# Second score pass of each head on half of the array's rows, one query block per half

## The chip, the core and the metric

The kernel runs on one core of a Trainium2 chip. The metric is the device time of one execution in microseconds (us); runs of the same kernel are summarised by their median. One profiled execution of the kernel gives the trace from which all rows come. TensorE is shown as two lines there: PE for the matmuls and PEld for the loads of the stationary operand ahead of each matmul. DVE is VectorE, ACT is ScalarE, POOL is GpSimd, SP is the queue that issues most DMAs.

## The reference: windowed attention, then a dense pair of layers

```
scores = (q @ k.T) / 8                       # batch 4, 8 heads, 768 positions, head size 64
keep   = (key < n_sink) | (0 <= query - key < window)    # 4 sinks, window 128
a      = softmax(where(keep, scores, -1e9))
x      = (a @ v) laid out as [3072 tokens, 512]
h      = x @ w_in                            # 512 -> 2048
out    = (max(h, 0) + log1p(exp(-|h|))) @ w_out   # 2048 -> 512
```

All inputs and outputs are float32.

## The kernel before

**Tiling.** The 3072 tokens are cut into 12 chunks of 256 (three per batch), each of two query blocks of 128 (`CH = 2`, index j). A chunk goes through eight heads of attention and then through eight slices of the dense layers. The attention of a chunk and the dense slices of the chunk before it are interleaved, so that each step holds one head and one slice.

**Precision.** Matmuls run on float32r, a rounded form of float32. To keep the accuracy, an operand is split into a high part (the rounded value) and a low part (what rounding left), and the products high·high, low·high and high·low are added up. The dense layers do this with three matmuls per tile (lines 495 and 546 to 548).

**The scores.** The head size is 64, and the array contracts over 128 rows, so the first two chunks (`EXACT = 2`) take plain float32 in another layout (line 257), while from the third chunk on a head's keys and queries are loaded twice, into rows 0 to 63 and into rows 64 to 127 of one tile of 656 columns (`load`, line 200): 400 columns of keys (previous block, sinks, own block, sinks, next block) and 256 columns of queries. `split` (line 204) then makes three things. ACT rounds the whole tile into `qkh` (line 210). DVE replaces the queries in the lower 64 rows of `qkh` by their low part (line 211, one subtraction of 64x256), so that a query column holds the high part over the low part. DVE writes the low part of the keys into `kl` on all 128 rows (line 213, 128x400). All these subtractions carry line 56, that of the helper `_sub`.

`scores` (line 246) then takes two passes for each query block j into the block's own PSUM tile `s`:

```
nc.tensor.matmul(s[:, :w], hi[:, st], hi[:, mv], start=True, stop=False)   # line 260
nc.tensor.matmul(s[:, :w], hi[:, st], kl[:, mv], start=False, stop=True)   # line 261
```

Line 260 gives (high + low query) times high key, line 261 gives (high + low query) times low key. Each is one weight load of 128 columns and one matmul that streams 264 columns, or 136 where j is the first block of a sequence (24 of 160 blocks). The order on PE is j=0 first and second pass, then j=1 first and second pass. With 10 chunks of 8 heads there are 80 heads, 160 matmuls of each line.

**What sets the order.** All engines issue in the order in which the program is emitted. The first two chunks and the preparation of the dense weights follow a list written out by hand (`START`). Then each step runs a fixed string of letters (`STEADY`): `k` sink weights, `W` the transposes of the softmax weights (line 329), `R`, `q`, `p` the `split` of the next head, `U` the 24 up-projection matmuls (line 495), `K` the sink transposes (line 313, every fourth step), `F`, `S` the scores, `T` the softmax, `D` six down-projection matmuls (lines 546 to 548), `P`, `N`, `V` the values (lines 362 and 369), `O`, `E` six more down-projection matmuls. So the scores stand between the up projection and the first half of the down projection, and the `split` of a head is emitted one step ahead of its scores.

**The softmax** (line 264) starts on DVE with a predicated copy that folds the window's two key blocks of `s` (line 275), then adds mask and scale (line 281). The PSUM pool of `s` has two tiles, one per block, so a head's scores wait for the softmax of the head before, a step earlier.

**A matmul of another shape.** In the constants, ahead of the first scores, line 113 spreads the two sizes over all partitions with a matmul whose stationary operand has one row. Around it stand the warm-up matmuls of line 660 (128 rows, on a tile of zeros) and the first scores of line 257 (128 rows).

Of the kernel before, what the change touches and what calls it, by code (L numbers as in the profile page):

```python
# [20 lines left out]
B, H, S, D = 4, 8, 768, 64  # L21
DM, DFF = 512, 2048
P = 128
# [3 lines left out]
CH = 2  # L27
CT = CH * P
KC = CH * KW + P
# [16 lines left out]
def _copy(nc, eng, out, in_):  # L46
    if eng == "A":
        nc.scalar.copy(out, in_)  # L48
    elif eng == "V":
        nc.vector.tensor_copy(out, in_)  # L50
    else:
        nc.gpsimd.tensor_scalar(out, in_, 1.0, 0.0, ALU.mult, ALU.add)


def _sub(nc, eng, out, a, b):
    (nc.vector if eng == "V" else nc.gpsimd).tensor_tensor(out, a, b, ALU.subtract)  # L56


def _zero(nc, out, finite):
    nc.gpsimd.tensor_scalar(out, finite, 0.0, 0.0, ALU.mult, ALU.add)  # L60
# [67 lines left out]
class _Attention:  # L128
# [75 lines left out]
    def split(self, h):  # L204
        if self.exact:
            return
        c, nc, chunk = self.c, self.c.nc, self.chunk
        r = self.heads[h]
        hi = c.lp.tile([P, QK], F32R, tag="qkh", name=f"qkh{chunk}_{h}")
        _copy(nc, c.E["qkh"], hi[:], r[:])  # L210
        _sub(nc, c.E["ql"], hi[D:, KC:], r[D:, KC:], hi[D:, KC:])
        kl = c.lp.tile([P, KC], F32R, tag="kl", name=f"kl{chunk}_{h}")
        _sub(nc, c.E["kl"], kl[:], r[:, :KC], hi[:, :KC])
        self.heads[h] = (hi, kl)
# [27 lines left out]
    def lone(self, j):  # L242

        return self.first and j == 0

    def scores(self, h):
        c, nc = self.c, self.c.nc
        ops = self.heads.pop(h)
        for j in range(CH):
            pool, tag = (c.ps_h, "h") if self.chunk == 0 and h % 2 else (c.ps_s, "s")  # L250
            s = pool.tile([P, 2 * P + NS], F32, tag=tag, name=f"s{self.chunk}_{h}_{j}")
            w = KW if self.lone(j) else 2 * P + NS
            mv = slice(j * KW, j * KW + w)
            st = slice(KC + j * P, KC + j * P + P)
            if self.exact:
                q, k = ops
                nc.tensor.matmul(s[:, :w], q[:, j * P : j * P + P], k[:, mv], start=True, stop=True)  # L257
            else:
                hi, kl = ops
                nc.tensor.matmul(s[:, :w], hi[:, st], hi[:, mv], start=True, stop=False)  # L260
                nc.tensor.matmul(s[:, :w], hi[:, st], kl[:, mv], start=False, stop=True)  # L261
            self.s[h, j] = s

    def softmax(self, h):
        c, nc, chunk = self.c, self.c.nc, self.chunk
        g, hh = h // G, h % G
        if hh == 0:
            self.a[g] = c.ap.tile([P, G, CH, KW], F32, tag="a", name=f"a{chunk}_{g}")
            self.rc[g] = c.sp.tile([P, CH, G], F32, tag="rc", name=f"rc{chunk}_{g}")
        sm = c.sp.tile([P, CH], F32, tag="sm", name=f"sm{chunk}_{h}")  # L270
        self.sm[h] = sm
        for j in range(CH):
            if self.lone(j):
                continue
            nc.vector.copy_predicated(self.s[h, j][:, :P], c.diag[:], self.s[h, j][:, KW:])
        for j in range(CH):
            a = self.a[g][:, hh, j]
            k = (chunk * H + h) * CH + j
            nm = c.stats[:, k : k + 1]
            m = c.masks[min(self.i0 + j, 2)]  # L280
            nc.vector.tensor_tensor_reduce(a, self.s.pop((h, j))[:, :KW], m[:], -SCALE, BIG, ALU.add, ALU.min, nm)  # L281
            nc.scalar.activation(a, a, AF.Exp, bias=nm, scale=-1.0, accum_out=sm[:, j : j + 1])  # L282
# [558 lines left out]
def _general(c):  # L841

    tc, nc = c.tc, c.nc
    with ExitStack() as st:
        pool = lambda n, bufs: st.enter_context(tc.tile_pool(name=n, bufs=bufs))
        psum = lambda n, bufs: st.enter_context(tc.tile_pool(name=n, bufs=bufs, space=bass.MemoryType.PSUM))
        c.stg, c.gp, c.xp, c.mp = pool("gstg", 2), pool("gp", 1), pool("gxp", 1), pool("gmp", 1)
        c.ps_acc, c.ps_h, c.gs, c.gt, c.gx = psum("gacc", 1), psum("gh", 1), psum("gs", 1), psum("gt", 1), psum("gx", 1)
        _general_weights(c)
        keep = _general_masks(c)  # L850
        with tc.For_i(0, B, 1) as b:
            for n in range(NCH):
                xh, xl = c.x[n] = [c.xp.tile([P, 4, CT], F32R, tag=f"x{e}", name=f"gx{e}{n}") for e in "hl"]
                for h in range(H):
                    if h % 2 == 0:
                        xt = c.gx.tile([P, CT], F32, name=f"g_x{n}_{h}", tag="g_x")
                    _general_head(c, b, n, h, keep, xt)
                    if h % 2 == 1:
                        _copy(nc, "A", xh[:, h // 2], xt[:])
                        _sub(nc, "V", xl[:, h // 2], xt[:], xh[:, h // 2])  # L860
                m = _Moe(c, n)
                m.row = b * S + n * CT
                for s in range(FP):
                    m.up(s)
                    m.softplus(s)
                    m.gate(s)
                    m.residue(s)
                    for j in range(2):
                        m.down(s, j)


def _kernel(tc, a, out):
    nc = tc.nc
    c = Ctx()
    c.nc, c.tc, c.a, c.out = nc, tc, a, out
    c.E = dict(qkh="A", ql="V", kl="V", vh="A", vl="P", xh="A", xl="P", gl="V", out="AV")
    c.x, c.vs, c.vst, c.vsr, c.vsh = {}, {}, {}, {}, {}
    c.w64 = a["w"].dtype == mybir.dt.int64
    nc.scalar.preload_act_table_set("natural_log_exp_and_others")
    with ExitStack() as keep:  # L880
        c.const = keep.enter_context(tc.tile_pool(name="const", bufs=1))
        c.wp = keep.enter_context(tc.tile_pool(name="wp", bufs=1))
        c.w, c.raw, c.top, c.word = {}, {}, {}, {}
        c.ident = c.const.tile([P, P], F32, name="ident")
        c.stats = c.const.tile([P, B * H * NB], F32, name="stats")
        c.room = c.const.tile([P, 2, 4 * FP], F32, name="room")
        nc.gpsimd.memset(c.room[:], 1.0)
        c.sk = c.const.tile([P, CT], F32R, name="sk")
        ones = c.room[:].rearrange("p a b -> p (a b)").unsqueeze(1).broadcast_to([P, CT // 64, 64])
        _zero(nc, c.sk[:].rearrange("p (a b) -> p a b", b=64), ones)  # L890
        with ExitStack() as st:
            pool = lambda n, bufs: st.enter_context(tc.tile_pool(name=n, bufs=bufs))
            psum = lambda n, bufs: st.enter_context(tc.tile_pool(name=n, bufs=bufs, space=bass.MemoryType.PSUM))
            c.xp, c.mp, c.stg = pool("xp", 2), pool("mp", 2), pool("stg", 4)
            c.lp, c.ap, c.sp = pool("lp", 2), pool("ap", 2), pool("sp", 2)
            c.ps_acc, c.ps_h = psum("ps_acc", 1), psum("ps_h", 2)
            c.ps_s, c.ps_t, c.ps_x = psum("ps_s", 2), psum("ps_t", 1), psum("ps_x", 1)
            c.last = True
            with tc.manual_schedule(engines=ORDERED):
                _fast(c)  # L900
            c.last = False
        ok = nc.values_load(c.flag[:1, :1], min_val=0, max_val=1)
        with tc.If(ok < 1):
            _general(c)
# [27 lines left out]
def build(nc, a, out):  # L932
    with tile.TileContext(nc, schedule_with_timeline_sim=True) as tc:
        _kernel(tc, a, out)
# [55 lines left out]
```

## Time and profile before

| | |
|---|---|
| median of three runs | 714.58 us (714.29 to 714.80) |
| the profiled execution | 714.26 us |
| its span, first to last instruction | 712.5 us |
| granted TensorE clock, mean | 0.999 |
| PE, PEld busy | 695.6, 627.4 us |
| DVE, ACT, POOL busy | 578.3, 452.9, 369.5 us |
| score passes of lines 260 and 261 | 160 matmuls each, from 69.5 to 625.3 us |
| their share of the chain that ended last | 3% each |

A matmul's row gives its start and a length that runs on until its last result is written, so neighbouring matmuls overlap in the rows: the distance between starts is what a matmul takes from the engine. The 1.8 us between span and execution time lie outside the first and last instruction.

### The profile page before, as it was taken

How to read it: one execution, taken by the hardware profiler on the slowest of the kernel's cores; microseconds unless marked ns; L12 is line 12 of the kernel's file. 1: busy time of each engine (PE TensorE's matmuls, PEld its weight loads, DVE VectorE, ACT ScalarE, POOL GpSimd, SP SyncE). 2: the span in 40 equal slices, each digit the busy share in tenths (PEclk: the TensorE clock that was granted, in tenths of full speed). 3: DMA queues.
4: the chain of work that ended last, by engine and by line, in shares of the span. 5: the costliest groups of instructions: out<-in, count | busy, mean ns of one | idle time of the engine just before them, and what ended most of it. 6: DMA issues, size and time to landing. Idle time of an engine off the chain costs nothing.

```text
span 712.5 us, 13842 instructions
## 1 busy us (share of the span) xinstructions
PE 695.6 (98%) x4536; PEld 627.4 (88%) x4536; DVE 578.3 (81%) x1657; ACT 452.9 (64%) x1113; POOL 369.5 (52%) x676
## 2 busy tenths in 40 slices
PE   8998899999999999999999999999999999999996
PEld 7887779899989989899998989999998989999995
DVE  7999999888888987887887887888888888865541
ACT  5879866657666666666666666666666765753431
POOL 6767457555554555565555655564554555542000
PEclk9999999999999999999999999999999999999999
DMA  9985523213122221311321321312222221100001
GB/s 321 372 325 207 168 71 100 63 59 94 46 80 80 69 67 61 102 46 47 111 59 50 109 69 51 108 49 65 81 71 69 80 75 55 61 12 1 30 2 34
DMA packets 39341, 64.52 MB, mean 91 GB/s; under 512 B 4508, under 2 KB 19932, under 8 KB 39260
## 3 DMA queue, kind: packets, MB, share of 16 engines
q1 hardware_dynamic: 38826, 63.02, 28.0%
q8 instruction: 38, 0.62, 0.4%
q10 hardware_dynamic: 434, 0.52, 0.2%
q14 instruction: 43, 0.35, 0.2%
HBM read 57.24 MB, written 6.29 MB: 89 GB/s over the span
## 4 chain that ended last, share of the span: by engine, by line
PE 90%; DVE 4%; ACT 3%; DMA 1%; issue 0%; POOL 0%; SPq 0%; ACTq 0%; POOLq 0%
PE h L495 37%; PE acc L546 12%; PE acc L547 12%; PE acc L548 12%; PE x L369 5%; PE s L260 3%; PE s L261 3%; PE t L329 3%; PE x L362 2%; DMA wo50r<-w 1%; ACT a L282 1%; PE word_ps L660 1%; PE ts L313 1%; ACT upper L48 1%; PE s L257 1%; DVE wt L439 1%
## 5 line engine op out<-in xcount | busy, mean ns | idle before, releaser
L495 PE MATMUL h<-xh,wi 128*128 128x256 f32 x1536 | 253.5, 287 | 0.4 <-DVE mt L510 0.4
L495 PEld LDWEIGHTS h<-xh,wi 128*128 128x128 f32 x1536 | 211.2, 191 | 1.7 <-DVE mt L510 0.6
L296 POOL TENSOR_SCALAR a<-a,rc 128x128 f32<-128x128 f32 x178 | 67.4, 391 | 184.0 <-DVE rc L289 156.4
L495 PE MATMUL h<-xl,wi 128*128 128x256 f32 x768 | 154.8, 283 | 1.6 <-DVE xl L56 1.6
L546 PE MATMUL acc<-wo,gh 128*128 128x512 f32 x384 | 152.3, 397 | 0.3 <-ACT gh L48 0.3
L548 PE MATMUL acc<-wo,gl 128*128 128x512 f32 x384 | 150.8, 393 | 0.3 <-DVE gl L56 0.3
L547 PE MATMUL acc<-wo,gh 128*128 128x512 f32 x384 | 151.0, 393 | 0.0
L495 PEld LDWEIGHTS h<-xl,wi 128*128 128x128 f32 x768 | 119.5, 192 | 2.0 <-DVE xl L56 2.0
L502 ACT ACTIVATE mt<-h 128x512 f32<-128x512 f32 x96 | 57.0, 594 | 98.7 <-PE h L495 98.7
L510 DVE SCALAR_TENSOR_TENSOR mt<-h,mt 128x512 f32<-128x512 f32 x96 | 66.1, 689 | 63.8 <-ACT mt L504 56.1
L282 ACT ACTIVATE a<-a,stats 128x136 f32<-128x136 f32 x192 | 76.1, 397 | 38.9 <-DVE stats L281 38.9
L548 PEld LDWEIGHTS acc<-wo,gl 128*128 128x128 f32 x384 | 72.1, 188 | 17.9 <-DVE gl L56 1.2
L546 PEld LDWEIGHTS acc<-wo,gh 128*128 128x128 f32 x384 | 72.1, 188 | 13.5 <-ACT gh L48 0.8
L547 PEld LDWEIGHTS acc<-wo,gh 128*128 128x128 f32 x384 | 72.3, 188 | 8.8
L56 DVE TENSOR_TENSOR gl<-mt,gh 128x512 fp32r<-128x512 f32 x96 | 79.1, 824 | 0.2
L340 POOL TENSOR_SCALAR_AFFINE_SELECT pt<-tl 128x256 fp32r<-128x256 f32 x80 | 59.1, 738 | 23.0 <-DVE tl L56 22.7
L340 POOL TENSOR_SCALAR_AFFINE_SELECT pt<-th 128x256 fp32r<-128x256 f32 (+1 forms) x96 | 46.4, 483 | 40.4 <-ACT th L48 38.8
L503 ACT ACTIVATE mt<-mt 128x512 f32<-128x512 f32 x96 | 60.8, 633 | 3.1
L504 ACT ACTIVATE mt<-mt 128x512 f32<-128x512 f32 x96 | 60.7, 633 | 3.0
L48 ACT CAST qkh<-qk 128x656 fp32r<-128x656 f32 x80 | 59.5, 744 | 0.4 <-DMA qk<-qk 0.4
L56 DVE TENSOR_TENSOR kl<-qk,qkh 128x400 fp32r<-128x400 f32 x80 | 51.5, 644 | 2.5
L56 DVE TENSOR_TENSOR tl<-t,th 128x256 f32<-128x256 f32 x80 | 33.2, 414 | 23.3 <-ACT th L48 23.3
(191 smaller groups left out, 1248.3 us busy)
## 6 DMA issues: line engine op xcount, KB each, us to landing
qk<-qk SPq DMA_DIRECT2D x160, 164.0 KB, 3.0
out<-o SPq DMA_DIRECT2D x23, 256.0 KB, 2.2
vr<-v SPq DMA_DIRECT2D x28, 192.0 KB, 2.5
q<-q SPq DMA_DIRECT2D x7, 256.0 KB, 5.6
k<-k SPq DMA_DIRECT2D x8, 200.0 KB, 8.1
vz<-v SPq DMA_DIRECT2D x4, 384.0 KB, 7.9
vr<-v SPq DMA_DIRECT2D x12, 128.0 KB, 2.1
vz<-v SPq DMA_DIRECT2D x4, 256.0 KB, 4.1
```

What stands on the lines that cost most here:

```text
L48: nc.scalar.copy(out, in_)
L56: (nc.vector if eng == "V" else nc.gpsimd).tensor_tensor(out, a, b, ALU.subtract)
L282: nc.scalar.activation(a, a, AF.Exp, bias=nm, scale=-1.0, accum_out=sm[:, j : j + 1])
L296: (nc.vector if eng == "V" else nc.gpsimd).tensor_scalar(a, a, rc[:, j : j + 1], 0.0, ALU.mult, ALU.add)
L340: nc.gpsimd.affine_select(pt[:, e, :, 1], src[:], [[0, CH], [1, P]], ALU.is_ge, 0.0, base=0, channel_multiplier=-1)
L495: nc.tensor.matmul(h[:, j], wt, x, start=k == 0, stop=k >= len(prods) - 2, skip_group_check=True)
L503: nc.scalar.activation(t[:], t[:], AF.Exp, scale=-1.0)
L504: nc.scalar.activation(t[:], t[:], AF.Ln, bias=1.0)
L510: nc.vector.scalar_tensor_tensor(t[:], h[:], 0.0, t[:], ALU.max, ALU.add)
L546: nc.tensor.matmul(acc[:], gh[:, j, q], wh, start=f == 0, stop=False, skip_group_check=True)
L547: nc.tensor.matmul(acc[:], gh[:, j, q], wl, start=False, stop=False, skip_group_check=True)
L548: nc.tensor.matmul(acc[:], gl[:, j, q], wh, start=False, stop=f == 2 * FP - 1, skip_group_check=True)
```

## The change

The second pass of a block contracts over 64 rows instead of 128: block 0 uses rows 0 to 63, block 1 rows 64 to 127. For that, the high part of a block's queries must lie in those rows, so the low part of block 1's queries goes into the upper rows and that of block 0 into the lower rows; the one subtraction of 64x256 becomes two of 64x128. The second pass then holds high query times low key only: low query times low key is no longer computed. Both second passes are emitted behind both first passes, so that the two stand next to each other.

```diff
@@ split
-        _sub(nc, c.E["ql"], hi[D:, KC:], r[D:, KC:], hi[D:, KC:])
+        for j in range(CH):
+            low = self.rows(1 - j), slice(KC + j * P, KC + j * P + P)
+            _sub(nc, c.E["ql"][j], hi[low], r[low], hi[low])
@@ new
+    def rows(self, half):
+        return slice(half * D, half * D + D)
@@ scores
+        parts = []
         for j in range(CH):
...
                 nc.tensor.matmul(s[:, :w], hi[:, st], hi[:, mv], start=True, stop=False)
-                nc.tensor.matmul(s[:, :w], hi[:, st], kl[:, mv], start=False, stop=True)
+                r = self.rows(j)
+                parts.append((s[:, :w], hi[r, st], kl[r, mv]))
             self.s[h, j] = s
+        for o, a, b in parts:
+            nc.tensor.matmul(o, a, b, start=False, stop=True)
@@ _kernel
-    c.E = dict(qkh="A", ql="V", kl="V", vh="A", vl="P", xh="A", xl="P", gl="V", out="AV")
+    c.E = dict(qkh="A", ql="VV", kl="V", vh="A", vl="P", xh="A", xl="P", gl="V", out="AV")
```

`"VV"` puts both subtractions on DVE, where the one was.

## Prediction

> **What bounds the kernel now.** I read the page first: busy times, the slices and the chain that ended last.
>
> ```profile
> PE 695.6 (98%) x4536; PEld 627.4 (88%) x4536; DVE 578.3 (81%) x1657; ACT 452.9 (64%) x1113; POOL 369.5 (52%) x676
> ...
> PE   8998899999999999999999999999999999999996
> ...
> DVE  7999999888888987887887887888888888865541
> ...
> PE 90%; DVE 4%; ACT 3%; DMA 1%; issue 0%; POOL 0%; SPq 0%; ACTq 0%; POOLq 0%
> ```
>
> PE is full in nearly every slice and makes up 90% of the chain. A busy PE row alone proves little, since matmuls overlap in the rows. So I asked for the sums of two stretches, and for who PEld waited for between 104 and 626 us.
>
> ```profile
> 60.00:120.00 60.00, 54.80 (x352) 48.32 (x351) 56.97 (x148) 46.27 (x109) 35.32 (x57) 1.00 0.40 122
> 400.00:500.00 100.00, 100.00 (x670) 91.10 (x670) 84.55 (x244) 64.93 (x161) 56.33 (x104) 1.00 0.23 66
> ...
> PEld ts L313 <- DVE tl L56: 0.7, 3, 0.2
> ```
>
> The last row is the only wait of that stretch: 0.7 us in 522. From 104 us on PE waits for nobody, DVE idles 15% of the time, ACT 35%. Before that PE has gaps: 5.2 us between 60 and 120. So what a head's scores gain or lose on PE goes into the span one to one, for every head behind 104 us. The scores themselves, in the timeline at 402 us (start, length):
>
> ```profile
> 401.98 0.29 PE L260 MATMUL s<-qkh 128*128 128x264 f32 x1
> 402.11 0.29 PE L261 MATMUL s<-kl,qkh 128*128 128x264 f32 x1
> 402.23 0.28 PE L260 MATMUL s<-qkh 128*128 128x264 f32 x1
> 402.36 0.28 PE L261 MATMUL s<-kl,qkh 128*128 128x264 f32 x1
> 402.48 0.39 PE L546 MATMUL acc<-wo,gh 128*128 128x512 f32 x1
> ...
> 401.99 0.19 PEld L261 LDWEIGHTS s<-kl,qkh 128*128 128x128 f32 x1
> 402.11 0.19 PEld L260 LDWEIGHTS s<-qkh 128*128 128x128 f32 x1
> ```
>
> A pass takes 0.12 to 0.13 us from start to start, a head's four 0.50 us until the down projection begins. The weight loads cost nothing, because each runs while the matmul ahead of it streams: that of the pass at 402.11 starts at 401.99, just behind the start of the matmul at 401.98. This cover is what the change puts at stake.
>
> **The change part by part: the array's shape.** Nothing of four passes goes away; two of them get 64 rows, and may run side by side. Four shapes of work follow each other in each head: 128 rows, 64 upper, 64 lower, 128 rows. Where does the trace show rows changing? At the first scores, where a one-row matmul (line 113) stands between 128-row ones:
>
> ```profile
> 4.83 0.33 PEld L660 LDWEIGHTS word_ps<-sk 128*128 128x128 f32 x1
> ...
> 5.04 0.33 PEld L660 LDWEIGHTS word_ps<-sk 128*128 128x128 f32 x1
> 5.60 0.28 PEld L113 LDWEIGHTS sizes_ps<-sizes_row,mask_room 1*128 1x128 f32 x1 [0.22 <-issue]
> ...
> 4.70 0.15 DVE L111 SCALAR_TENSOR_TENSOR sizes_row<-words_top,words_f 1x2 f32<-1x2 f32 x1
> ...
> 5.25 0.41 PE L660 MATMUL word_ps<-sk 128*128 128x256 f32 x1
> ...
> 5.76 0.33 PEld L113 LDWEIGHTS sizes_ps<-sizes_row,mask_room 1*128 1x128 f32 x1
> 5.83 0.35 PE L113 MATMUL sizes_ps<-sizes_row,mask_room 1*128 1x2 f32 x1
> ...
> 6.11 0.29 PEld L257 LDWEIGHTS s<-k,q 128*128 128x128 f32 x1
> ```
>
> The warm-up loads come 0.21 us apart, each at the start of the matmul ahead. The load of the one-row matmul should have come at 5.25, but starts at 5.60, 0.35 later. It did not wait for data: what it reads was done on DVE at 4.85, and the profile puts the idle time to "issue", to nothing that it shows. The last 128-row matmul ends at 5.66. On the way back it is the same: the one-row matmul ends at 6.18, and the 128-row load starts at 6.11 and not at the one-row matmul's start. So a load of another row count starts about 0.07 us before the modelled end of the last matmul: the array runs empty first. It is not the change of operands or number format, for where line 660 meets line 257 again, both on 128 rows, the load is back at the start of the matmul ahead:
>
> ```profile
> 8.07 0.28 PE L660 MATMUL word_ps<-sk 128*128 128x256 f32 x1
> ...
> 8.08 0.19 PEld L257 LDWEIGHTS s<-k,q 128*128 128x128 f32 x1
> ```
>
> The Trainium skill, "TensorEngine Tiling (Array Packing)", section Tiling Modes under Key Properties, says that changing the tiling mode, not just the tile, drains TensorE, which speaks against this change; it gives no time for it, and the rows above agree with 0.35 us at half the clock.
>
> What an empty array then costs, at the clock of the scores, is shown where a load had waited for DVE:
>
> ```profile
> 72.92 0.19 PEld L548 LDWEIGHTS acc<-wo,gl 128*128 128x128 f32 x1 [0.70 <-DVE gl L56]
> ...
> 73.03 0.19 PEld L546 LDWEIGHTS acc<-wo,gh 128*128 128x128 f32 x1
> ...
> 72.92 0.50 PE L548 MATMUL acc<-wo,gl 128*128 128x512 f32 x1 [0.27 <-DVE gl L56]
> 73.26 0.40 PE L546 MATMUL acc<-wo,gh 128*128 128x512 f32 x1
> ```
>
> The next load follows 0.11 after the first, so a load holds its port for 0.11 us, and the matmul streams only after it: 73.26 less the 0.23 of a 512-wide matmul is 73.03 again.
>
> **The sum of a head.** Count from the start of block 0's first pass. Block 1's first pass starts at 0.12 (row 401.98 to 402.11). Its length is 0.28, so the array is free for the half-row load at 0.12 + 0.28 - 0.07 = 0.33. The load takes 0.11: the first half-row pass streams from 0.44. The second one's load follows at 0.44 and its pass streams from 0.55. That ends at 0.83 by the row's length; the down projection's load starts at 0.76, and its matmul streams from 0.87. Before, that was 0.50. A head is 0.37 us longer, and behind the waiting load stand, on PE, the two half-row passes, all 12 down matmuls and the values of that step, with nothing to do meanwhile.
>
> Bounds. Drain: the 0.07 could shrink with the clock to 0.035, which gives 0.04 more per switch; or the array empties 0.13 after the stream's end at half clock (5.25 + 0.21 to 5.60), so 0.065 at full clock behind 0.11 of streaming, 0.18 instead of 0.21. Two switches: -0.06 to +0.08. Second half-row load: nothing, if halves load side by side, to 0.11; no two loads on different halves stand in the trace, and the nearest pair, at 72.92 and 73.03, is 0.11 apart, so I take 0.11. In 24 heads block 0 streams 136 columns and not 264; the loads, which set the steps behind the drain, are as long there, so the sum stays. A head comes to 0.20 to 0.45 us, with 0.37 as the value.
>
> Heads: five begin before 104 us, where PE's gaps (5.2 us in that stretch) can swallow 0.37 each, so they count nothing; 75 count in full. 75 x 0.37 = 27.8 us, bounds 75 x 0.20 = 15 and 80 x 0.45 = 36.
>
> **DVE.** One subtraction becomes two of half the width:
>
> ```profile
> L56 DVE TENSOR_TENSOR kl<-qk,qkh 128x400 fp32r<-128x400 f32 x80 | 51.5, 644 | 2.5
> L281 DVE CUSTOM_DVE_ANT_0 a<-s,mask 128x136 f32<-128x136 f32 x192 | 49.0, 291 | 0.6
> L56 DVE TENSOR_TENSOR qkh<-qk,qkh 64x256 fp32r<-64x256 f32 x80 | 40.9, 511 | 2.6 <-ACT qkh L48 0.2
> L275 DVE COPY_PREDICATED s<-diag,s 128x128 f32<-128x128 int32 x160 | 39.8, 282 | 1.2 <-PE s L261 1.1 <-PE s L257 0.2
> ...
> L261 PEld LDWEIGHTS s<-kl,qkh x160: 187/188/193, 69.6 to 625.2; 128*128 128x128 f32 x160
> ...
> L56 DVE TENSOR_TENSOR kl<-qk,qkh x80: 574/664/872, 65.7 to 619.0; 128x400 fp32r<-128x400 f32 x80
> ```
>
> 511 and 644 ns for 256 and 400 columns are 0.92 ns a column, so 393 for 128; the row of 128 columns nearest by form, line 275, has 282. The pair costs 564 to 786, that is 0.05 to 0.28 us more per head, 4 to 22 us of DVE in all. Its cover: DVE idles 15.45 us in the 100 from 400 on, about 1.1 us for each head's 7 us (75 heads in 522), and the last of these subtractions starts at 619.0 while the pass that reads it loads at 625.2, six microseconds later. So I count nothing; gone, it would cost 0.28 x 75 = 21 us at most. Line 275 gets its scores 0.3 us later than now; it waited for them for 1.1 us in all, in two places, so DVE mostly comes later than that. No DMA, no POOL or ACT instruction is added or moved.
>
> Sum: 714.26 + 27.8 = 742.0 for the profiled execution, 0.3 under the median of the runs, so **742.3 us** for the median. What this kernel's measurement can tell from no change is 0.2%, 1.4 us.
>
> **The rivals.** *The passes overlap and the switch is free (faster).* If the half-row loads run ahead under the 128-row pass as all loads do now, the two half-row passes share one pass's time. Limited by the load port, the down projection starts 0.11 after the second half-row pass, whose load comes 0.11 after the first one's: 0.46 instead of 0.50, 80 x 0.04 = 3 us, 711. If loads of different halves run side by side too, a whole pass of 0.12 goes: 80 x 0.12 = 9.6 us, 705. It decides from the point where both switches together cost under 0.12 us. For it: nothing in the trace shows 64 rows, and one place with one row at half the clock is thin. Against it: that place shows the wait on both sides. By the Trainium skill, "TensorE: Matmul & The Clock Gate", Part 3, matmuls on different row groups start about 4 ns apart, which is the 705; no run here shows it. Chance 0.14.
>
> *The loads run ahead and only the matmul waits for the empty array.* The half-row passes stream from 0.12 + 0.18 to 0.25, together, and the down projection as much later: 0.48 to 0.62, so -0.02 to +0.12 a head, 713 to 723. Against it: at 5.60 and 6.11 it is the load that waits. Chance 0.10, of which 0.08 slower and 0.02 the same.
>
> *No other shape at all.* The half-row passes use the array like full ones, one after the other: four passes at 0.12, 714.6. The one-row load speaks against it. Chance 0.05.
>
> **How the numbers follow.** The drain with loads behind it keeps 0.71, at 742.3 with 729 to 751 of its own, a little more if each switch also waits for the last result's full end (0.07 more, 75 x 0.14 = 10 us). Slower 0.71 + 0.08 = 0.79, same 0.02 + 0.05 = 0.07, faster 0.14. The range leaves out the faster rival and the far end of the first case: 714 to 753.
>
> **What would show it.** In the changed profile: the half-row load starts 0.2 us behind the start of block 1's first pass, not at it; the two half-row loads stand 0.11 apart, or start together; the down projection's first load starts 0.2 us behind the start of the second half-row stream; four passes take 0.87 instead of 0.50; PEld shows idle time put to "issue" at these two loads, some 0.15 us each; up and down matmuls keep their 0.12 and 0.23; DVE's busy time grows by 4 to 22 us with no new wait of PE for DVE. It is wrong if the loads run on without a gap at the switch, or if PE starts waiting for `kl` or `qkh`.

## Result and profile after

The changed kernel takes 734.07 us in the median (733.54 to 734.88, four runs) against 714.43 us beside it: 19.6 us or 2.8% slower, ratio 1.0277, 95% interval 1.0264 to 1.029. The forecast was 742.3 us in a range of 714 to 753.

The page of the profile after, the lines that answer to those of before:

```profile
span 733.2 us, 13923 instructions
...
PE 717.6 (98%) x4536; PEld 627.9 (86%) x4536; DVE 588.0 (80%) x1737; ACT 452.2 (62%) x1113; POOL 371.0 (51%) x676
...
PE   8998999999999999999999999999999999999996
...
PE 88%; ACT 2%; DVE 2%; issue 0%; ACTq 0%
```

PE has as many instructions as before, is as full in every slice, and yet is busy 22 us longer; DVE has 80 instructions and 9.7 us more. PE still waits for nobody, as the waits of PEld from 104 to 645 us show:

```profile
PEld h L505 <- DVE xl L56: 0.6, 1, 0.6
PEld s L272 <- issue: 0.5, 3, 0.2
```

Two rows, 1.1 us in 541: the time went into PE's own sequence. The timeline of one head (line 267 is the first pass, 272 the half-row pass, 556 and 557 the down projection), weight loads first, then matmuls:

```profile
435.89 0.31 PEld L267 LDWEIGHTS s<-qkh 128*128 128x128 f32 x2
436.34 0.19 PEld L272 LDWEIGHTS s<-kl,qkh 64*128 64x128 f32 x2
436.66 0.19 PEld L556 LDWEIGHTS acc<-wo,gh 128*128 128x128 f32 x1
436.77 0.19 PEld L557 LDWEIGHTS acc<-wo,gh 128*128 128x128 f32 x1
...
436.13 0.29 PE L267 MATMUL s<-qkh 128*128 128x264 f32 x1
...
436.01 0.41 PE L267 MATMUL s<-qkh 128*128 128x264 f32 x2
436.34 0.39 PE L272 MATMUL s<-kl,qkh 64*128 64x264 f32 x2
436.66 0.50 PE L556 MATMUL acc<-wo,gh 128*128 128x512 f32 x1
437.00 0.39 PE L557 MATMUL acc<-wo,gh 128*128 128x512 f32 x1
```

Read the loads against the matmuls. Block 1's first pass starts at 436.13; before, the next load came with it. Now it comes at 436.34, 0.21 later. Both half-row loads together fill 0.19 us, the length of one: they run side by side, and so do their matmuls (two in 0.39). The load of the down projection comes at 436.66, and the load behind it is 0.11 later. A 512-wide matmul takes 0.23, so line 556 streams from 437.00 - 0.23 = 436.77. From the first pass at 436.01 that is 0.76 us; before it was 0.50. Longer by 0.26 a head; 75 heads make 19.5 us, and 19.6 were measured. Summed over the matmul starts of the two traces, the 75 heads behind 104 us take 20.2 us longer (0.27 each), of the 20.7 between the two spans.

### The profile page after: what moved, and what is told of

Same layout as the page of the kernel before. It is cut to its first block, busy times and chain, and to the rows that moved or that the text cites. A ratio compares the mean times of both kernels' runs of the same rounds, so it can differ in the third digit from the quotient of the medians.

```text
span 733.2 us, 13923 instructions
## 1 busy us (share of the span) xinstructions
PE 717.6 (98%) x4536; PEld 627.9 (86%) x4536; DVE 588.0 (80%) x1737; ACT 452.2 (62%) x1113; POOL 371.0 (51%) x676
## 4 chain that ended last, share of the span: by engine, by line
PE 88%; ACT 2%; DVE 2%; issue 0%; ACTq 0%
PE h L505 35%; PE acc L556 14%; PE acc L558 12%; PE acc L557 12%; PE x L379 5%; PE s L272 3%; PE s L267 3%; PE t L339 2%; PE x L372 1%; PE ts L323 1%; ACT upper L48 1%; DVE wt L449 0%; DVE wo L56 0%; ACT wo L48 0%; DVE sm L298 0%
## 5 line engine op out<-in xcount | busy, mean ns | idle before, releaser
L556 PE MATMUL acc<-wo,gh 128*128 128x512 f32 x384 | 160.7, 418 | 0.0
L557 PE MATMUL acc<-wo,gh 128*128 128x512 f32 x384 | 150.6, 392 | 0.0
L513 ACT ACTIVATE mt<-mt 128x512 f32<-128x512 f32 x96 | 60.7, 633 | 3.1
L514 ACT ACTIVATE mt<-mt 128x512 f32<-128x512 f32 x96 | 60.7, 633 | 3.1
L56 DVE TENSOR_TENSOR qkh<-qk,qkh 64x128 fp32r<-64x128 f32 x160 | 60.7, 379 | 2.3
L56 POOL TENSOR_TENSOR vv<-vr,vv 128x384 fp32r<-128x384 f32 (+1 forms) x40 | 55.9, 1397 | 0.0
```

Source lines behind the costliest of these rows:

```text
L513: nc.scalar.activation(t[:], t[:], AF.Exp, scale=-1.0)
L514: nc.scalar.activation(t[:], t[:], AF.Ln, bias=1.0)
L556: nc.tensor.matmul(acc[:], gh[:, j, q], wh, start=f == 0, stop=False, skip_group_check=True)
L557: nc.tensor.matmul(acc[:], gh[:, j, q], wl, start=False, stop=False, skip_group_check=True)
```

## Experiments

The theory: each change between 128 and 64 rows lets the array run empty before the next weight load may start, 0.20 us a switch, and two switches a head cost more than the one pass that the two halves share. Rivals: the new order of the passes costs; the cut subtraction on DVE costs; 64-row passes are slow in themselves.

**The order alone.** From the kernel before:

```diff
-                nc.tensor.matmul(s[:, :w], hi[:, st], kl[:, mv], start=False, stop=True)
+                parts.append((s[:, :w], hi[:, st], kl[:, mv]))
             self.s[h, j] = s
+        for o, p, m in parts:
+            nc.tensor.matmul(o, p, m, start=False, stop=True)
```

> Only the order is changed: both first passes, then both second passes, all four on 128 rows, one subtraction as before. Drain theory (each change between 128 and 64 rows makes the next weight load wait until the array is empty, and this alone lengthens the kernel): no change, 714.4 us within 0.2%. Rival 'order' (the later block 0 or the alternation of the two PSUM tiles is what costs): some or all of the 19.6 us, up to 734.

Measured: 714.27 us, ratio 0.9997 (0.9988 to 1.0006). The order costs nothing that can be told from the noise.

**The cut subtraction alone.** From the kernel before:

```diff
-        _sub(nc, c.E["ql"], hi[D:, KC:], r[D:, KC:], hi[D:, KC:])
+        for j in range(CH):
+            low = slice((1 - j) * D, (2 - j) * D), slice(KC + j * P, KC + j * P + P)
+            _sub(nc, c.E["ql"], hi[low], r[low], hi[low])
```

> Only the subtraction is cut in two (block 1's low part in the upper rows, block 0's in the lower); the four passes stand in the old order on 128 rows. Drain theory: DVE gets about 10 us more work, PE waits for none of it, 714.4 us within 0.2%. Rival 'DVE' (the added DVE work delays what PE waits for): slower, up to 734.

Measured: 713.59 us, ratio 0.9992 (0.9983 to 1.0001). Its page has DVE at 585.5 us, 7.2 above before, and no time comes of it. Both rivals on what stands around the passes are out.

**Both half-row passes on the same half.** From the changed kernel:

```diff
-            low = self.rows(1 - j), slice(KC + j * P, KC + j * P + P)
+            low = self.rows(1), slice(KC + j * P, KC + j * P + P)
...
-                r = self.rows(j)
+                r = self.rows(0)
```

> As the changed kernel, but both second passes use rows 0 to 63 (one subtraction's worth of low parts in the lower rows for both blocks), so they can't run side by side. Drain theory: the two switches stay and the overlap of one pass goes: 0.12 us more for each of some 78 heads, 9.4 us over the changed kernel's 734.1, 743.5 us; the second half-row weight load starts 0.11 or more behind the first and not 3 ns behind it. If the side-by-side passes gain nothing in the changed kernel: 734.

Measured: 742.83 us, ratio 1.0396 (1.038 to 1.0412), 8.8 us over the changed kernel. The timeline of a head:

```profile
442.10 0.29 PEld L272 LDWEIGHTS s<-kl,qkh 64*128 64x128 f32 x2
442.54 0.19 PEld L556 LDWEIGHTS acc<-wo,gh 128*128 128x128 f32 x1
...
441.77 0.41 PE L267 MATMUL s<-qkh 128*128 128x264 f32 x2
442.11 0.50 PE L272 MATMUL s<-kl,qkh 64*128 64x264 f32 x2
442.54 0.50 PE L556 MATMUL acc<-wo,gh 128*128 128x512 f32 x1
442.88 0.40 PE L557 MATMUL acc<-wo,gh 128*128 128x512 f32 x1
```

The two loads now fill 0.29 us, so the second starts 0.10 to 0.11 behind the first, and the two matmuls 0.50 where they filled 0.39. The head takes 442.88 - 0.23 - 441.77 = 0.88 us. This is the head that the prediction summed (0.87), and the time that it gave. Here both passes start at row 0, and the switches cost what they did, so it is not the start at row 64 that costs.

**Four switches.** From the changed kernel, each half-row pass back behind its own first pass:

```diff
-                parts.append((s[:, :w], hi[r, st], kl[r, mv]))
+                nc.tensor.matmul(s[:, :w], hi[r, st], kl[r, mv], start=False, stop=True)
             self.s[h, j] = s
-        for o, a, b in parts:
-            nc.tensor.matmul(o, a, b, start=False, stop=True)
```

> As the changed kernel, but each half-row pass stands behind its own block's first pass: 128, 64, 128, 64 rows, four switches in a head and no overlap. Drain theory: a lone half-row pass costs two switches of 0.20 us, so a head is 0.80 us longer than before; 75 heads, 60 us, 774 us. Rival 'half-row passes are slow in themselves': the number of switches doesn't matter and losing the overlap adds 0.12, about 744. Rival 'order': the order is the old one, 714 to 720.

Measured: 769.39 us, ratio 1.0768 (1.0751 to 1.0784). The loads of a head (line 266 first pass, 268 half-row pass, 553 down projection):

```profile
457.15 0.19 PEld L266 LDWEIGHTS s<-qkh 128*128 128x128 f32 x1
457.48 0.18 PEld L268 LDWEIGHTS s<-kl,qkh 64*128 64x128 f32 x1
457.80 0.19 PEld L266 LDWEIGHTS s<-qkh 128*128 128x128 f32 x1
458.12 0.18 PEld L268 LDWEIGHTS s<-kl,qkh 64*128 64x128 f32 x1
458.43 0.19 PEld L553 LDWEIGHTS acc<-wo,gh 128*128 128x128 f32 x1
```

Where rows change, a load comes 0.31 to 0.33 behind the one ahead of it, and not 0.12 as between passes of one shape: 0.19 to 0.21 for each switch, and it shows at all four of them. The cost goes with the number of switches, and the old order does not save it. Four of them are 0.78 us in this head. The kernel is 55.2 us over the one before and not the expected 60, and the traces show where the rest went. By the matmul starts, 51 of the 75 heads behind 104 us grow by 0.77 us; the other 24, whose block 0 streams 136 columns and not 264, grow by 0.68: 55.8 us in all. The loads of such a head, from block 0's half-row pass on:

```profile
319.42 0.18 PEld L268 LDWEIGHTS s<-kl,qkh 64*128 64x128 f32 x1
319.67 0.19 PEld L266 LDWEIGHTS s<-qkh 128*128 128x128 f32 x1
319.99 0.18 PEld L268 LDWEIGHTS s<-kl,qkh 64*128 64x128 f32 x1
320.31 0.19 PEld L553 LDWEIGHTS acc<-wo,gh 128*128 128x128 f32 x1
```

Behind the half-row pass of 136 columns the next load comes after 0.25 us, behind that of 264 columns after 0.32. The wait follows the length of the stream ahead of it, as it must if the array has to run empty, and is not a fixed time for each switch.

**96 rows.** From the changed kernel:

```diff
-                r = self.rows(j)
-                parts.append((s[:, :w], hi[r, st], kl[r, mv]))
+                parts.append((s[:, :w], hi[:96, st], kl[:96, mv]))
```

> As the changed kernel in order and subtractions, but both second passes contract over rows 0 to 95, which is neither a half nor the whole (the sum of products differs from the kernel's: for block 0 a part of the low query is taken in, for block 1 half of the high query is left out). Drain theory with whole-array shapes: 96 rows are run as the whole array, no switch, 714.4 us. Drain theory by the exact row count: two switches and no overlap, 743. Rival 'fewer rows are slow in themselves': between.

Measured: 713.91 us, ratio 0.9997 (0.9987 to 1.0007). The loads of a head:

```profile
423.62 0.31 PEld L267 LDWEIGHTS s<-qkh 128*128 128x128 f32 x2
423.86 0.31 PEld L271 LDWEIGHTS s<-kl,qkh 96*128 96x128 f32 x2
424.10 0.19 PEld L555 LDWEIGHTS acc<-wo,gh 128*128 128x128 f32 x1
```

Pairs start 0.24 apart, 0.12 a load, with no gap at 96 rows. So another row count alone does not empty the array. That 64 rows use it in another division than 128 do, and 96 rows the undivided one, fits this run and the halves that load side by side; the traces show the times alone, and no row count between 64 and 96 was run.

**Four pairs in one visit, and the control on 128 rows.** The changed kernel with

```diff
-        for o, a, b in parts:
-            nc.tensor.matmul(o, a, b, start=False, stop=True)
+        for e in range(4):
+            for o, a, b in parts:
+                nc.tensor.matmul(o, a, b, start=False, stop=e == 3)
```

and, for the control, `hi[:, st], kl[:, mv]` in place of `hi[r, st], kl[r, mv]`.

> As the changed kernel, but the pair of half-row second passes is issued four times over into the same tiles (low keys are added four times, so the sum differs): one visit to the 64-row shape with four pairs. Drain theory: the visit's 0.40 us stay, each further pair costs one pass of 0.12 us: 734.1 + 78 x 3 x 0.12 = 762 us. Rival 'half-row passes are slow in themselves' (each pair costs what the first did, 0.24 + 0.27 us): 734.1 + 78 x 3 x 0.51 = 853 us.

> The control of the run with four pairs: the same order and the same eight second passes, all on 128 rows (low keys added four times). No switch; six more passes of 0.122 us in each of 80 heads: 714.4 + 58.6 = 773 us. So by the drain theory four pairs in one visit are where half rows win, by about 11 us; by the rival they lose by 80.

Measured: half rows 762.52 us, ratio 1.0676 (1.0657 to 1.0695); full rows 767.59, ratio 1.0756 (1.0737 to 1.0775). The matmuls of a head with four half-row pairs:

```profile
452.57 0.41 PE L267 MATMUL s<-qkh 128*128 128x264 f32 x2
452.90 0.75 PE L273 MATMUL s<-kl,qkh 64*128 64x264 f32 x8
453.58 0.50 PE L557 MATMUL acc<-wo,gh 128*128 128x512 f32 x1
```

and with eight full passes:

```profile
456.18 0.41 PE L267 MATMUL s<-qkh 128*128 128x264 f32 x2
456.42 1.15 PE L272 MATMUL s<-kl,qkh 128*128 128x264 f32 x8
457.40 0.40 PE L556 MATMUL acc<-wo,gh 128*128 128x512 f32 x1
```

Between the first and the next line's start stand 0.68 us for four half-row pairs (452.90 to 453.58) against 0.32 for one pair in the changed kernel (436.34 to 436.66): 0.12 for each further pair, as the theory had it, and what one full pass takes ((457.40 - 456.42) / 8 = 0.12). So 64-row passes are not slow in themselves, and with four pairs in a visit the half rows win, by 5.1 us where 11 were expected. The control is what came out shorter, by 5 us. Its trace shows why. The sixth head starts at 111.0 us where it started at 110.2 before, so of the extra passes of the five early heads (3.7 us at the 0.73 that a later head grows by) only 0.8 us is left, and the rest lies in PE's gaps. The 24 heads with 136 columns in block 0 grow by 0.70 and not by 0.73, which is another 0.9 us.

No version here beats the kernel before: the ones without a switch measure the same as it.

## Why the prediction was right, point by point

- *What bounds the kernel.* Right. PE waited for nobody before and after, and what the heads gained went into the span.
- *A load of another shape waits until the array is empty.* Right for 64 rows between 128, and shown by four switches, by the passes of 136 columns and by the gaps at each load. It carried over from one matmul of one row, in a place where matmuls of 256 columns started 0.21 us apart and not 0.12. The prediction calls that half the clock; the profile's clock row shows 1.00 from 4.5 to 6.2 us, so the slower pace is what the trace shows, not its cause. As the prediction words it, for "another row count", the rule is too wide: 96 rows do not wait. That 64 rows would do as one row did could not be read from that row.
- *Size of the drain.* Right. Taken was a load 0.28 - 0.07 = 0.21 behind the start of the pass ahead; measured 436.34 - 436.13 = 0.21. At the way out, 0.21 behind the start of the stream was taken; the half-row stream starts one load (0.11) after 436.34, at 436.45, and the next load comes at 436.66: 0.21. The idle time put to "issue" that was to show it appears only three times (0.5 us); the gaps stand in the rows, where the loads of the first passes end at 435.89 + 0.31 = 436.20 and the next comes at 436.34.
- *The second half-row load at 0.11.* This is the term that was mis-sized: "nothing, if halves load side by side, to 0.11", and 0.11 was taken because the nearest pair of loads, both on 128 rows, was that far apart. On different halves they load together, as the prediction had it in one of its rivals but not in its sum. With nothing in its place the prediction's own sum is 0.26 a head, 75 x 0.26 = 19.5, 733.8 for the profiled execution. The run with both passes on one half, where the loads are 0.11 apart, gave 742.83 us against the forecast 742.3. So this one term, 75 x 0.11, is the 8.2 us by which the forecast was too high.
- *The early heads.* Roughly right: the heads before 104 us counted for nothing in the sum, and the profiled span grew by 20.7 us, of which the 75 later heads have 20.2.
- *DVE.* Right that nothing comes of it: 9.7 us more in the bounds of 4 to 22, and the cut alone left the time as it was. The total hides two parts: the two subtractions take 60.7 us where the one took 40.9, near the upper bound, and that of the low keys behind them takes 6.8 us less, which the prediction had not counted. That the step behind the scores mostly comes later than they do held too, but less than before: line 285 (275 before) now waits for the half-row pass in 22 of 160 places, 6.1 us, where it was two and 1.1 us.

```profile
L272 PEld LDWEIGHTS s<-kl,qkh x160: 182/183/184, 70.4 to 646.2; 64*128 64x128 f32 x160
...
  DVE s L285: 6.1, 22
```

  These 6.1 us lie in DVE's idle time, and PE does not wait for DVE longer than before.
- *The rivals.* The free switch is out by every run. Loads that run ahead, with only the matmul waiting, are out by the rows: it is the load that comes late. "No other shape" is out too, since two half-row matmuls fill the time of one.

## What to carry to other kernels

Where PE never waits for another engine, as here, running matmuls on halves of the array side by side saves one pass for each pair, 0.12 us here, and costs two switches, 0.40 us for each visit; so four pairs in a row paid, and one pair between full-array matmuls is a loss. By the same numbers two pairs would lose and three come out about even (0.40 against 0.36); neither was run. Before packing, look in the trace for any matmul of another row count and see whether its weight load still starts with the matmul ahead of it; a wait there is a warning and no proof, since 96 rows have none. Where the pairs can't be collected (here each pair needs two PSUM tiles of scores), passes of 96 or 128 rows, which pay no switch, are the cheaper ones.

## What the runs showed of the hardware that was not expected

- Two weight loads on different halves start together and take 0.183 us each, as one load does; on the same half the second is 0.11 behind. The Trainium skill, "TensorE: Matmul & The Clock Gate", Part 3, says that matmuls on different row groups run concurrently in the same array. These rows agree (two such matmuls fill 0.39 us, and one alone is 0.38 long); the trace of before could not show it.
- A contraction over 96 rows between 128-row ones leaves no gap, and takes 0.12 us as they do.
- The low part of the keys, the same subtraction of 128x400 in each kernel, took 644 ns before, 558 after (558 or 559 in each run with one low part in either half) and 880 in the run with both low parts in the lower rows. Rows of the groups after, then of that run:

```profile
L56 DVE TENSOR_TENSOR kl<-qk,qkh 128x400 fp32r<-128x400 f32 x80 | 44.7, 558 | 0.0
```

```profile
L56 DVE TENSOR_TENSOR kl<-qk,qkh 128x400 fp32r<-128x400 f32 x80 | 70.4, 880 | 2.5
```

  It is shortest where the subtraction ahead of it starts in the upper rows, as it does itself. The cause was not tried by itself.
